# Opening a fused attention and dense kernel with a quarter of q loaded in fp32 by SyncE, k by heads, and both z groups ahead of kv

## The chip, the cores and the metric

The kernel runs on one core of a Trainium2 chip. The metric is the device time of one execution in microseconds (us). Each kernel was executed four or five times, with executions of the kernel before on the same chip in the same rounds. A profile is a trace of one of these executions; its span is about 1.8 us shorter than that execution's time. "Before" and "after" are the two kernels; of the 18 experiments, each has one profile, so a single start or landing time below is that of one execution.

Five engines appear. TensorE multiplies matrices, ScalarE computes exp and tanh, VectorE the other elementwise work; GpSimd and SyncE start loads here. A load is started ("issued") by an engine and carried out by 16 DMA engines; it has "landed" when its data may be used.

## The reference

```python
def phi(x):
    return np.where(x > 0, x, np.exp(x) - 1.0) + 1.0
q_p, k_p = (phi(q), phi(k))                      # q, k, v: (8 batches, 8 heads, 576, 64) fp32
kv = np.einsum('bhsd,bhse->bhde', k_p, v)
z = np.sum(k_p, axis=2)
num = np.einsum('bhsd,bhde->bhse', q_p, kv)
den = np.einsum('bhsd,bhd->bhs', q_p, z)[..., None] + 1e-06
attn = num / den
x = attn.transpose(0, 2, 1, 3).reshape(4608, 512)
h = x @ w_in                                     # 512 x 2048
g = h - np.tanh(h)
out = g @ w_out                                  # 2048 x 512, fp32
```

Linear attention over eight batches gives 4608 tokens; two dense layers follow. phi is computed as min(exp(x), max(x, 0) + 1): an exp on ScalarE, a max and a min on VectorE.

## The kernel before

All inputs are loaded by GpSimd, because they are cast from fp32 to bf16 on the way. They stand in one queue, called the stream here: q, k and v of batch 0 in two halves each, the slices of w_in, then k of batch 1, half of w_out, q of batch 1 (called q(1) here), v of batch 1, the rest of w_out.

```python
def load(b, t, src, halves):
    x = src[b].rearrange("h (p j) d -> (h p) (j d)", j=J)
    if halves:                                   # batch 0: two loads of 256 rows
        for i in range(2):
            nc.gpsimd.dma_start(out=t[:, :, i].rearrange("q h j d -> q h (j d)"),
                                in_=x.rearrange("(h i q) x -> i q h x", h=2, i=2)[i])
    else:
        nc.gpsimd.dma_start(out=t.rearrange("q h i j d -> q (h i) (j d)"), ...)
...
load_q(0)
load_k(0)
make_identity(nc, ident)
load_v(0)
for f0, n in ((0, 256), (256, 256), (512, 512), (1024, 512), (1536, 512)):
    load_wi(f0, n)
load_k(1)
load_wo(0)
load_wo(1)
load_q(1)
...
load_v(1)
load_wo(2)
load_wo(3)
```

The opening computes the attention of batch 0, in this order; `spin` is matmuls on zeros that fill TensorE's waits.

```python
(eq0, rq0, mq0), (eq1, rq1, mq1) = (phi_pieces(0, q_t, qp_t, "qp", i) for i in range(2))
for f in (eq0, rq0, mq0, eq1, rq1, mq1):         # exp, max, min of each half of q
    f()
spin(18)
a_qT_pe(0, 0, side, "AV")                        # transposes of phi(q), first half
...
for f in (ek0, rk0, *ek1, mk0, rk1):
    f()
spin(5)
a_qT_pe(0, 1, side, "AA")
...
b0_z(0)                                          # z of the first half of k
for f in mk1:
    f()
b0_zc(0)                                         # its product with the mask, on VectorE
b0_kv(0)                                         # kv of half the heads; needs v
b0_kz(0)
b0_z(1)                                          # z of the second half of k
b0_zc(1)
a_den(0, Banks([4]))                             # denominators and their reciprocal
...
```

Then come nine chunks of 512 tokens, each with 64 matmuls by w_in and 64 by w_out. In the second layer of the first chunk stand the transposes of phi(q) of batch 1 and, after them, the kv matmuls of batch 1:

```python
s2[3].append(lambda: a_qphi(1, 0))
s2[4].append(lambda: (a_qphi(1, 1), load_q(2), load_k(2), load_v(2)))
...
s2[7].append(lambda: (a_qT_pe(1, 0, side), a_qT_pe(1, 1, side), a_kv(1, side)))
```

## Time and profile before

| what | value |
|---|---|
| time, median of 3 runs | 295.44 us (295.11 to 295.5) |
| span of the profile | 293.2 us |
| TensorE busy | 285.2 us, 97% |
| first dense matmul / start of the long dense run | 16.38 / 17.64 us |
| q(1) landed | 35.92 us |
| kv matmuls of batch 1 start | 39.78 us |

TensorE is the bound, so the opening matters only by how far left it lets TensorE's long run start. The prediction shows the chain of loads, and TensorE at 38 us. The timeline of ScalarE (start, length, engine, line, operation, out<-in, and how many instructions are put together; in brackets the idle time before it and what ended it) tells when the two halves of q land:

```profile
5.55 1.16 ACT L134 ACTIVATE e<-qraw 128x1152 bf16<-128x1152 bf16 x1 [3.32 <-DMA qraw<-in_q_dram]
6.90 1.16 ACT L134 ACTIVATE e<-qraw 128x1152 bf16<-128x1152 bf16 x1 [0.19 <-DMA qraw<-in_q_dram]
```

The timeline of TensorE has the two starts of dense work; between them it makes the last two pairs of batch 0:

```profile
16.38 0.59 PE L366 MATMUL ps_all<-xT,w_in_sb 128*128 128x512 bf16 x2 [0.33 <-DVE xT L244]
16.98 0.73 PE L240 MATMUL ps_all<-rden,sel 32*128 32x128 f32 x16
17.64 13.55 PE L366 MATMUL ps_all<-xT,w_in_sb 128*128 128x512 bf16 x62
```

From 17.64 on TensorE runs without a wait until the transposes at 37.94.

### The profile page before, as it was taken

How to read it: one execution, taken by the hardware profiler on the slowest of the kernel's cores; microseconds unless marked ns; L12 is line 12 of the kernel's file. 1: busy time of each engine (PE TensorE's matmuls, PEld its weight loads, DVE VectorE, ACT ScalarE, POOL GpSimd, SP SyncE). 2: the span in 40 equal slices, each digit the busy share in tenths (PEclk: the TensorE clock that was granted, in tenths of full speed). 3: DMA queues.
4: the chain of work that ended last, by engine and by line, in shares of the span. 5: the costliest groups of instructions: out<-in, count | busy, mean ns of one | idle time of the engine just before them, and what ended most of it. 6: DMA issues, size and time to landing. Idle time of an engine off the chain costs nothing.

```text
span 293.2 us, 4504 instructions
## 1 busy us (share of the span) xinstructions
PE 285.2 (97%) x1801; PEld 134.3 (46%) x1801; DVE 174.6 (60%) x265; ACT 139.6 (48%) x168; POOL 33.3 (11%) x55
## 2 busy tenths in 40 slices
PE   8899999999999999999999999999999999999994
PEld 2544453454444444444444445444444444444443
DVE  4759857887567764786478646865581456106600
ACT  4938536947344643455246524661552155126411
POOL 8673030030030003000300020000000000000000
PEclk9999999999999999999999999999999999999999
DMA  6999999998999758955895669667117310131032
GB/s 101 194 204 212 208 207 216 200 145 153 234 163 185 160 118 139 218 117 129 136 223 127 139 134 183 134 154 143 38 24 178 73 36 0 38 84 24 0 74 72
DMA packets 39077, 38.94 MB, mean 133 GB/s; under 512 B 16336, under 2 KB 33808, under 8 KB 38288
## 3 DMA queue, kind: packets, MB, share of 16 engines
q0 software_dynamic: 17552, 18.35, 38.6%
q1 hardware_dynamic: 21344, 20.17, 30.3%
q8 instruction: 14, 0.23, 0.3%
q10 hardware_dynamic: 160, 0.13, 0.1%
q14 instruction: 7, 0.06, 0.1%
HBM read 43.91 MB, written 9.55 MB: 182 GB/s over the span
## 4 chain that ended last, share of the span: by engine, by line
PE 79%; DMA 11%; issue 7%; POOL 2%; DVE 0%; ACT 0%; POOLq 0%
PE ps_all L387 37%; PE ps_all L366 36%; DMA qraw<-in_q_dram 6%; DMA w_in_sb<-in_moe_w_in_dram 3%; PE ps_all L199 2%; DMA kraw<-in_k_dram 2%; PE ps_all L317 2%; PE ps_all L604 1%; PE ps_all L276 1%; POOL qraw L90 0%; ACT e L134 0%; POOL kraw L93 0%; DVE qp L136 0%; POOL v L93 0%; POOL w_out_sb L115 0%
## 5 line engine op out<-in xcount | busy, mean ns | idle before, releaser
L366 PE MATMUL ps_all<-xT,w_in_sb 128*128 128x512 bf16 x576 | 128.0, 379 | 0.3 <-DVE xT L244 0.3
L387 PE MATMUL ps_all<-w_out_sb,gT 128*128 128x512 bf16 x560 | 127.8, 379 | 0.0
L373 DVE TENSOR_TENSOR gT<-ps_all,th 128x1024 bf16<-128x1024 f32 x64 | 77.9, 1218 | 59.8 <-ACT th L372 59.8
L372 ACT ACTIVATE th<-ps_all 128x1024 f32<-128x1024 f32 x64 | 65.5, 1024 | 57.0 <-PE ps_all L366 47.1
L366 PEld LDWEIGHTS <-w_in_sb 128*128 128x128 bf16 x576 | 55.3, 98 | 66.6 <-issue 0.6
L387 PEld LDWEIGHTS <-gT 128*128 128x128 bf16 x560 | 54.1, 98 | 64.3 <-issue 0.3
L396 ACT COPY osb<-ps_all 128x512 f32<-128x512 f32 (+1 forms) x36 | 20.9, 583 | 73.4 <-PE ps_all L387 54.2
L328 DVE TENSOR_TENSOR xT<-ps_all,rdb 128x512 bf16<-128x512 f32 x24 | 16.3, 689 | 13.4 <-PE ps_all L317 11.2
L134 ACT ACTIVATE e<-qraw 128x1152 bf16<-128x1152 bf16 x16 | 18.5, 1162 | 6.9 <-DMA qraw<-in_q_dram 6.9
L134 ACT ACTIVATE e<-kraw 128x1152 bf16<-128x1152 bf16 x15 | 17.5, 1166 | 0.2 <-DMA kraw<-in_k_dram 0.2
L136 DVE TENSOR_TENSOR qp<-e,r 128x1152 bf16<-128x1152 bf16 x16 | 12.0, 757 | 7.8 <-ACT e L134 7.2
L136 DVE TENSOR_TENSOR kp<-e,r 128x1152 bf16<-128x1152 bf16 x15 | 11.4, 759 | 8.3 <-ACT e L134 7.5
L383 POOL COPY g<-qT 1x1 bf16<-1x1 bf16 x5 | 1.2, 240 | 120.6 <-DMA qT<-qp 120.6
L378 DVE TENSOR_TENSOR gT<-ps_all,th 128x512 bf16<-128x512 f32 x16 | 10.3, 685 | 2.4 <-ACT th L377 1.7
L377 ACT ACTIVATE th<-ps_all 128x512 f32<-128x512 f32 x16 | 9.2, 598 | 4.3 <-PE ps_all L366 3.1
L317 PE MATMUL ps_all<-qT,kz 128*128 128x512 bf16 x28 | 10.1, 379 | 0.0
L444 PE MATMUL ps_all<-zero 128*128 128x512 bf16 x29 | 8.8, 463 | 1.2 <-DVE zero L405 1.2
L135 DVE TENSOR_SCALAR r<-qraw 128x1152 bf16<-128x1152 bf16 x16 | 7.3, 453 | 2.2 <-DMA qraw<-in_q_dram 2.2
L199 PE MATMUL ps_all<-vp,kp 64*128 64x136 bf16 x216 | 7.4, 220 | 0.4 <-POOL g L383 0.4
L199 PEld LDWEIGHTS <-kp 64*128 64x128 bf16 x216 | 6.4, 94 | 3.0 <-issue 2.1
L285 DVE RECIPROCAL rden<-den 128x144 f32<-128x144 f32 x7 | 7.4, 1053 | 0.2
L394 DVE COPY osb<-ps_all 128x128 f32<-128x128 f32 x1 | 0.3, 292 | 11.6 <-PE ps_all L604 11.6
(82 smaller groups left out, 121.7 us busy)
## 6 DMA issues: line engine op xcount, KB each, us to landing
out_dram<-osb SPq DMA_DIRECT2D x70, 128.0 KB
rdb<-ds SPq DMA_DIRECT2D x12, 576.0 KB
kraw<-in_k_dram POOLq DMA_DIRECT2D x7, 576.0 KB, 7.1
qraw<-in_q_dram POOLq DMA_DIRECT2D x7, 576.0 KB, 9.0
v<-in_v_dram POOLq DMA_DIRECT2D x7, 576.0 KB, 12.2
w_out_sb<-in_moe_w_out_dram POOLq DMA_DIRECT2D x4, 512.0 KB, 16.4
w_in_sb<-in_moe_w_in_dram POOLq DMA_DIRECT2D x6, 256.0 KB, 8.6
qraw<-in_q_dram POOLq DMA_DIRECT2D x2, 288.0 KB, 4.6
```

The lines of the kernel that those rows point to most:

```text
L134: return (lambda: nc.scalar.activation(e, x, AF.Exp), lambda: nc.vector.tensor_scalar(r, x, 0.0, 1.0, ALU.max, ALU.add), lambda: nc.vector ...
L136: lambda: nc.vector.tensor_tensor(y, e, r, ALU.min))
L199: nc.tensor.matmul(ps[hg][:, i, :], kp[r, i, j].rearrange("p h d -> p (h d)"), vp[r, i, j, :], start=(j == 0), stop=(j == J - 1))
L317: nc.tensor.matmul(ps, kz[:, p // 2, p % 2, 0:128], qT[:, p % 2, 0:8, p // 2, :], start=True, stop=True)
L328: nc.vector.tensor_mul(xT[:, p, S * b:S * b + 512].rearrange("p (j t c) -> p j t c", j=8, t=4), ps.rearrange("p j (t c) -> p j t c", t=4), ...
L366: nc.tensor.matmul(h, w_in_sb[:, 2 * (p % 2) + p // 2, fi * 128:(fi + 1) * 128], xT[:, p, c * 512:(c + 1) * 512], start=(n == 0), stop=(n ...
L372: nc.scalar.activation(th, h, AF.Tanh)
L373: nc.vector.tensor_sub(gT[:, fi:fi + 2, :], h, th)
L377: nc.scalar.activation(th, h, AF.Tanh)
L378: nc.vector.tensor_sub(gT[:, fi, :], h, th)
L387: nc.tensor.matmul(o, gT[:, fi, i * 128:(i + 1) * 128], w_out_sb[:, fi, :], start=(fi == 0), stop=(fi == NF - 1))
L396: nc.scalar.copy(osb[:, f0:f1], o[:, f0:f1])
```

## The change

The intent is to start phi(q) earlier, with a piece that an idle engine loads while GpSimd has not yet begun, and to take the wait for v out of the way of the denominators. A quarter of q (128 of 512 rows of batch 0) is loaded by SyncE in fp32 into a buffer that is free until the first dense layer. GpSimd's first load is the other quarter of that half. The second half of k becomes two loads, by heads. phi(q)'s first half is done in two pieces. Both z groups and their mask products come before kv.

```diff
@@ load
+                if t is k_t.get(0) and i == 1:
+                    for h in range(2):
+                        nc.gpsimd.dma_start(out=t[:, h, i].rearrange("q j d -> q (j d)"),
+                                            in_=x.rearrange("(h i q) x -> h i q x", h=2, i=2)[h, i])
+                    continue
+                if t is q_t.get(0) and i == 0:
+                    nc.sync.dma_start(out=q_f, in_=x.rearrange("(h i q) x -> h i q x", h=2, i=2)[0, 0])
+                    nc.gpsimd.dma_start(out=t[:, 1, i].rearrange("q j d -> q (j d)"),
+                                        in_=x.rearrange("(h i q) x -> h i q x", h=2, i=2)[1, 0])
+                    continue
... (phi_pieces: exp, max and min by pieces)
@@ opening
+    q_f = gpool.tile([128, NF, 512], BF16, name="gT").rearrange("p a b -> p (a b)").bitcast(F32)[:, 0:J * D]
...
-    for f in (eq0, rq0, mq0, eq1, rq1, mq1):
+    for f in (eq0[0], rq0[0], eq0[1], rq0[1], *mq0, eq1, rq1, mq1):
         f()
-    spin(18)
+    spin(14)
...
-    for f in (ek0, rk0, *ek1, mk0, rk1):
+    for f in (ek0, rk0, *ek1, mk0):
         f()
...
-    spin(6)
+    spin(5)
     b0_z(0)
-    for f in mk1:
-        f()
+    for h in range(2):
+        rk1[h]()
+        mk1[h]()
     b0_zc(0)
+    b0_z(1)
+    b0_zc(1)
     b0_kv(0)
     b0_kz(0)
-    b0_z(1)
-    b0_zc(1)
     a_den(0, Banks([4]))
```

## The prediction

> **What bounds the kernel now.** I began with the page's busy shares: TensorE is at 97% of the span. The timeline of TensorE shows where the other 3% is: after the first dense matmuls it hardly stops until the last outputs, so a change in the opening can only shift that long run to the left. The question is what fixes its place. So I read the chain of work that ended last, in order of time, for the first 60 us:
>
> ```profile
> 1.24 1.33 POOL qraw L90 x2
> ...
> 2.78 6.16 DMA kraw<-in_k_dram
> ...
> 9.22 9.06 DMA w_in_sb<-in_moe_w_in_dram
> ...
> 18.57 0.74 POOL w_out_sb L115
> ...
> 19.39 16.51 DMA qraw<-in_q_dram
> ...
> 35.92 1.17 ACT e L134
> 37.12 0.76 DVE qp L136
> ```
>
> The columns are start, length, what. From 2.78 to 35.92 us it is nearly all loads: the opening, and the first dense stage too, hang on the stream of loads that GpSimd issues, of which the last that matters is q of batch 1, landing at 35.92. I checked this against TensorE's timeline at that place:
>
> ```profile
> 33.83 4.26 PE L387 MATMUL ps_all<-w_out_sb,gT 128*128 128x512 bf16 x19
> 37.94 0.68 PE L164 MATMUL ps_all<-ident,qp 128*128 128x128 bf16 x9
> 39.17 0.68 PE L164 MATMUL ps_all<-ident,qp 128*128 128x128 bf16 x9 [0.56 <-DVE qp L136]
> ```
>
> TensorE arrives at the first transposes of batch 1 at 37.94; their input was ready at 37.88. The second nine wait 0.56 us for the second half of phi(q). So slack here is zero, and the place of everything after 39.17 is the landing of q(1) plus 3.25 us of exp, max, min. The third view is the busy time by windows (the last four columns that matter are the clock, the DMA share and GB/s):
>
> ```profile
> 2.50:2.75 0.25, 0.25 (x2) 0.10 (x1) 0.21 (x7) 0.00 (x0) 0.25 (x1) 1.00 0.00 0
> 2.75:3.00 0.25, 0.25 (x2) 0.12 (x1) 0.25 (x3) 0.00 (x0) 0.25 (x2) 1.00 1.05 60
> 3.00:3.50 0.50, 0.50 (x3) 0.18 (x2) 0.35 (x5) 0.00 (x0) 0.50 (x2) 1.00 0.66 30
> 3.50:4.00 0.50, 0.50 (x3) 0.15 (x1) 0.00 (x0) 0.00 (x0) 0.50 (x2) 1.00 0.89 147
> 4.00:4.50 0.50, 0.50 (x2) 0.15 (x1) 0.00 (x0) 0.00 (x0) 0.45 (x2) 1.00 1.22 210
> ...
> 30.00:34.00 4.00, 4.00 (x20) 1.80 (x19) 3.90 (x8) 2.54 (x5) 0.00 (x0) 1.00 1.22 208
> 34.00:38.00 4.00, 4.00 (x20) 1.72 (x19) 2.94 (x13) 2.08 (x2) 0.00 (x0) 1.00 1.22 206
> ```
>
> Nothing moves before 2.75, little until 3.5, and from 4 us to 38 us the rate is flat at about 205 GB/s. It is a full pipe: q(1) lands when all that was queued ahead of it has passed. The rate counts bf16 written; the loads cast, so about 410 GB/s of fp32 is read.
>
> **What the Trainium skill says.** "DMA: Bandwidth & Descriptors", section "SWDGE vs HWDGE vs iDMA": a DMA that casts must come from GpSimd. This is why the quarter of q that SyncE loads has to stay fp32. The same page, "Specifications": first-byte latency about 1 us from GpSimd, 0.6 us from SyncE or ScalarE, and a fabric ceiling of 435 GB/s. The trace has 1.5 us from GpSimd (issue 1.24, first bytes in the window from 2.75) and 1.1 us for the last output (issued by SyncE at 288.99, bytes in the window from 290.00); the order agrees, the sizes are larger, and I use the trace's. The 410 GB/s read agrees with a pipe near that ceiling. Same page, "Issuing engines are not separate DMA queues": all issuers share the 16 engines and interleave. So SyncE brings no bandwidth here; it can only fill time in which the engines are empty. "VectorE: DVE Perf Modes", "The perf-mode tier table": tensor_scalar on fp32 drops from the 4x to the 2x mode; no instruction of before's profile shows this one.
>
> **The change part by part.**
>
> (1) Quarter of q by SyncE. 128 rows of 2304 bytes, read and written as fp32, in place of 128 rows that GpSimd's stream would have read and cast. In read bytes the pipe carries the same; written bytes go up by 144 KB, which I take as free because the flat rate looks read-bound. One such quarter takes 144 KB / 205 GB/s = 0.72 us of the pipe. The first instructions of the other engines start at 0.73 (ScalarE) to 0.86 (VectorE), GpSimd's DMA at 1.24. If SyncE issues at 0.75 to 0.9, its bytes start at about 1.9 to 2.3, 0.5 to 0.9 us before GpSimd's 2.78, and ramp through the empty stretch up to 3.5. Full hiding is worth 0.72 us, hiding half of it 0.36; with a ramp of its own of some 0.8 us (2.75 to 3.5 for GpSimd's) I take 0.6 us. Every later load, q(1) among them, then lands 0.6 us earlier: q(1) at 35.3.
>
> (2) k of the second half by heads. Two DMAs of 144 KB for one of 288. GpSimd's issue costs 0.74 us for 288 KB and, I estimate, about 0.6 us for a small one, so some 0.5 us more of issue; the issue of v (4.77) is far ahead of its landing (11.89), so it is hidden. The gain is that the first exp of that half may start before all has landed.
>
> (3) phi(q) first half in two pieces: exp 0.67 us each (as the two pieces of k, mean 675 ns) for 1.16, so 0.18 us more on ScalarE; the VectorE max in two pieces, the fp32 one about 0.35 us, min twice 0.42 for 0.76: some 0.2 us more. They start earlier than the 5.55 of now by 0.9 us or more, so this is hidden.
>
> (4) Both z groups ahead of kv. In before kv waits until 11.89 for v, and holds the second z back: z 12.39, its mask product 12.95 to 13.16, reciprocal 13.58. With loads 0.6 us earlier: k first half 8.35; exp to 9.5; min to 10.3; then VectorE runs max 0.25 and min 0.42 twice, to 11.6. Second z 11.6 to 12.0, kv (v landed at 11.3) to 12.45, the 20 denominator matmuls 0.25 + 0.4 to 13.1. Reciprocal 13.1 against 13.58; and 2.80 us from there to the first dense matmul as now: 15.9 against 16.38. The opening itself gains about 0.5 us. The order alone gains nothing unless k is ready before v lands, because the 0.45 us of kv then merely follows.
>
> (5) Five spins fewer (4 + 1): they only fill waits; 0.22 us each when warm, so 14 end near 6.2, where I expect the transposes.
>
> The sum is not (1) + (4): the opening's 0.5 us and the stream's 0.6 us meet at 37.94 to 39.17. TensorE comes there 0.5 us earlier, q(1) 0.6 us earlier; the second transposes still wait for it (gap 0.56 to about 0.46), and the net is the gain of q(1)'s landing, 0.6 us. Beyond 39.17 everything is relative to TensorE. 295.44 - 0.6 = 294.84.
>
> **Rivals.** (a) The opening's whole gain counts, 1 us or more: the removed waits (0.4 for v, 0.4 of the reciprocal for the denominator, the split of k) add up, and the time is 294.2. Against it: zero slack at 37.94; TensorE's gain beyond q(1)'s is returned there as a longer wait. (b) The SyncE load starts late: its first DMA is cold, and the write of the reciprocals issued at 14.66 needed until 20.14 for its readers to go, under load. Then the stream still loses 128 rows but phi(q) waits for SyncE; gain 0 to 0.3, time 295.2 to 295.4. For it: only unloaded cases at the end show 1.1 us. (c) VectorE becomes the opening's bound through eight small pieces in place of five, or the fp32 rows cost the pipe double, 0.7 us: then both are lost and the time is 295.4 to 295.7. Against: both sit in a phase with idle VectorE, and the pipe's rate follows read bytes.
>
> **Range and chances.** The three runs of before spread over 0.4 us, so I can tell 0.6 from 0 only just. (b) and (c) set the high end, 295.4; (a) with a fully hidden quarter the low end, 294.2. Two per cent is 5.9 us, ten times anything in this argument: "within 2%" is nearly certain.
>
> **What would show it.** Right: bytes moving by 2.3 us; the first exp at about 4.3 and not 5.55; the first dense matmul near 15.9; q(1) landed at 35.3; the transposes of batch 1 again waiting for phi(q), and everything after moved by the landing's gain. Wrong: q(1) landing at 35.9 in spite of an early SyncE load (the pipe is not read-bound), or the transposes of batch 1 without a wait (then the opening sets the end), or new gaps of TensorE between 16 and 38 us, at a dense matmul whose weights came late.

## The result, and the profile after

The changed kernel took 295.69 us (median of 4 runs, 295.27 to 296.19); the kernel before 295.27 in the same rounds (4 runs). The ratio is 1.0017, with a 95% interval of 0.9996 to 1.0039. A ratio is always the mean time of one kernel's runs over that of the other's runs of the same rounds, so it isn't quite the ratio of the medians. "Within 2%" held. The predicted gain of 0.6 us did not come, and 295.69 lies above the predicted range.

The chain of work that ended last, after, for the first 60 us (start, length, what):

```profile
1.91 6.18 DMA qraw<-in_q_dram
8.11 1.17 ACT e L147
9.31 0.76 DVE qp L149
...
13.40 0.39 PE ps_all L223 x18
13.79 0.53 PE ps_all L234 x18
...
18.91 2.49 PE ps_all L379 x11
```

Before, this chain ran through loads up to q(1) at 35.92. Now it leaves the loads at 8.11, with the second half of q, and goes through the opening's compute into the dense run. In the page's shares of the chain by engine the loads fall from 11% of the span to 4% (first before, then after):

```profile
PE 79%; DMA 11%; issue 7%; POOL 2%; DVE 0%; ACT 0%; POOLq 0%
PE 77%; issue 7%; DVE 6%; DMA 4%; ACT 3%; POOL 1%; SPq 0%; DVEq 0%; ACTq 0%; POOLq 0%
```

So something else bounds the start than the prediction had. ScalarE's timeline says where it begins:

```profile
3.77 0.68 ACT L143 ACTIVATE e<-gT 128x576 bf16<-128x576 f32 x1 [1.54 <-DMA gT<-in_q_dram]
5.45 0.68 ACT L143 ACTIVATE e<-qraw 128x576 bf16<-128x576 bf16 x1 [1.00 <-DMA qraw<-in_q_dram]
8.11 1.16 ACT L147 ACTIVATE e<-qraw 128x1152 bf16<-128x1152 bf16 x1 [1.98 <-DMA qraw<-in_q_dram]
...
35.47 2.22 ACT L147 ACTIVATE e<-qraw 128x1152 bf16<-128x1152 bf16 x2 [1.73 <-DMA qraw<-in_q_dram]
```

The SyncE quarter is there at 3.77, earlier than predicted. But the second half of q, which GpSimd loads, comes at 8.11 and not at 6.90: 1.21 us later, although a quarter of q has been taken out of the stream in front of it. Much further down the same stream, q(1) lands at 35.47, 0.45 us earlier than before. TensorE's timeline answers both:

```profile
17.58 0.38 PE L379 MATMUL ps_all<-xT,w_in_sb 128*128 128x512 bf16 x1 [0.33 <-DVE xT L257]
18.18 0.73 PE L253 MATMUL ps_all<-rden,sel 32*128 32x128 f32 x16 [0.23 <-DVE xT L257]
18.84 13.55 PE L379 MATMUL ps_all<-xT,w_in_sb 128*128 128x512 bf16 x61
32.23 7.07 PE L400 MATMUL ps_all<-w_out_sb,gT 128*128 128x512 bf16 x31
39.14 1.17 PE L177 MATMUL ps_all<-ident,qp 128*128 128x128 bf16 x18
40.37 1.66 PE L190 MATMUL ps_all<-v,kp 64*128 64x192 bf16 x36
```

The start of the dense work is 1.20 us later (17.58 for 16.38, 18.84 for 17.64). The eighteen transposes of batch 1 now run in one piece, with no wait for phi(q): the gap of 0.56 us is gone, because q(1) came early and TensorE late. So 1.20 of delay less about 0.6 of gap leave the kv matmuls of batch 1 at 40.37 instead of 39.78, 0.59 us later, and the span is 0.6 us longer.

The two profiles suggest a rule for the start of these kv matmuls: the later of *long dense run + 21.52* (after: 18.84 + 21.52 = 40.36) and *q(1) landing + 3.86* (before: 35.92 + 3.86 = 39.78). The constants were read from these two profiles. In both, the span is that start plus 253.4. The experiments will test it.

The windows of the two kernels (window, its length, busy time of PE, PEld, DVE, ACT and POOL with their counts, clock, DMA share, GB/s written) show what the stream did. Before:

```profile
2.50:3.50 1.00, 1.00 (x4) 0.40 (x3) 0.82 (x12) 0.00 (x0) 1.00 (x3) 1.00 0.59 30
3.50:4.50 1.00, 1.00 (x4) 0.30 (x2) 0.00 (x0) 0.00 (x0) 0.95 (x3) 1.00 1.05 179
4.50:8.00 3.50, 3.21 (x19) 1.43 (x18) 1.59 (x3) 2.26 (x2) 3.47 (x6) 1.00 1.17 190
8.00:12.00 4.00, 3.55 (x47) 1.98 (x46) 3.20 (x7) 3.45 (x6) 2.07 (x4) 1.00 1.19 198
```

After:

```profile
2.50:3.50 1.00, 1.00 (x4) 0.40 (x3) 0.82 (x12) 0.00 (x0) 1.00 (x3) 1.00 0.95 242
3.50:4.50 1.00, 1.00 (x4) 0.30 (x2) 0.46 (x1) 0.68 (x1) 1.00 (x3) 1.00 1.06 146
4.50:8.00 3.50, 2.77 (x20) 1.40 (x19) 1.15 (x3) 0.68 (x1) 3.06 (x6) 1.00 1.09 147
8.00:12.00 4.00, 2.32 (x31) 1.10 (x30) 2.96 (x6) 3.89 (x6) 2.44 (x4) 1.00 1.18 195
```

The empty time before 3.5 us is filled, as intended. But from 4.5 to 8 us the rate is 147 GB/s and not 190. That is 43 GB/s x 3.5 us = 150 KB not moved, about what the quarter of q (144 KB in bf16) had saved the stream; that the two are so near is chance, as the second profile of the same kernel shows (159 GB/s, so 109 KB). The column before the rate is the time that the DMA engines' packets took, as a share of the window. It falls only from 1.17 to 1.09 while the rate falls from 190 to 147, so in after the same bytes took about a fifth more packet time. That speaks against engines that merely had nothing to move.

The trace's packet records show one thing more. A load ends with sixteen 4-byte packets, and the Trainium skill ("DMA: Bandwidth & Descriptors", section "Why a DMA increments its semaphore by 16 and not by 1") says that for a load from GpSimd each of the 16 DMA engines posts a completion, and that the load has landed only when all have. In before the sixteen completions of GpSimd's first load lie within 0.35 us. In after fourteen lie within 0.46 us, and the next two come 1.31 and 1.46 us after the first. So the consumers seem to wait for one or two engines that lag by about a microsecond. The records don't name the engine, so which completion belongs to which load is read from their order. Where an engine lags by more than a whole load this order fails: in after the 32nd completion, which would be the last of GpSimd's second load, comes at 7.17, but the exp that needs that load starts only at 8.11, where in before it starts 0.3 to 0.4 us after its load's last completion.

### The profile page after: what moved, and what is told of

It is laid out like the page before. It is cut to its first block, busy times and chain, and to the rows that moved or that the text cites. A ratio compares the mean times of both kernels' runs of the same rounds, so it can differ in the third digit from the quotient of the medians.

```text
span 293.8 us, 4473 instructions
## 1 busy us (share of the span) xinstructions
PE 281.9 (96%) x1767; PEld 133.5 (45%) x1796; DVE 175.5 (60%) x268; ACT 139.5 (47%) x169; POOL 33.5 (11%) x56
## 4 chain that ended last, share of the span: by engine, by line
PE 77%; issue 7%; DVE 6%; DMA 4%; ACT 3%; POOL 1%; SPq 0%; DVEq 0%; ACTq 0%; POOLq 0%
PE ps_all L379 36%; PE ps_all L400 34%; DVE gT L391 2%; PE ps_all L212 2%; DMA out_dram<-osb 2%; DMA qraw<-in_q_dram 2%; PE ps_all L330 2%; ACT th L390 1%; PE ps_all L289 1%; DVE r L148 1%; ACT osb L409 1%; DVE kp L149 1%; DVE qp L149 1%; PE ps_all L253 0%; SPq L414 0%
## 5 line engine op out<-in xcount | busy, mean ns | idle before, releaser
L400 PE MATMUL ps_all<-w_out_sb,gT 128*128 128x512 bf16 x547 | 126.3, 379 | 0.7
L147 ACT ACTIVATE e<-qraw 128x1152 bf16<-128x1152 bf16 x15 | 17.3, 1162 | 3.7 <-DMA qraw<-in_q_dram 3.7
L149 DVE TENSOR_TENSOR qp<-e,r 128x1152 bf16<-128x1152 bf16 x15 | 11.3, 757 | 6.9 <-ACT e L147 6.2
L459 PE MATMUL ps_all<-zero 128*128 128x512 bf16 x24 | 7.3, 458 | 1.2 <-DVE zero L418 1.2
```

The costliest lines, as they stand in the source:

```text
L147: return (lambda: nc.scalar.activation(e, x, AF.Exp), lambda: nc.vector.tensor_scalar(r, x, 0.0, 1.0, ALU.max, ALU.add), lambda: nc.vector ...
L149: lambda: nc.vector.tensor_tensor(y, e, r, ALU.min))
L400: nc.tensor.matmul(o, gT[:, fi, i * 128:(i + 1) * 128], w_out_sb[:, fi, :], start=(fi == 0), stop=(fi == NF - 1))
```

## The experiments

All 18 runs gave correct results.

### e1: the change again

The unchanged file of after, to see how far one profile stands for the kernel.

> The changed kernel again, unedited, for a second profile. Theory S (the SyncE load disturbs GpSimd's stream) and theory H (loads of 128 rows instead of 256 are slow): the pattern repeats: second half of q lands after 7.7 us (before: 6.9), the first dense matmul starts near 17.6 (before: 16.4), q of batch 1 lands at 35.3 to 35.6, time 0.2 to 0.6 us over before. Theory A (an accident of the one profiled execution): second half of q by 6.9, first dense matmul near 16.

Measured: 295.48 us against 294.96; ratio 1.0016 (1.0000 to 1.0031). Of what was expected for a repeated pattern only the time held (0.2 to 0.6 us over). This execution's second half of q was there at 7.10, not 8.11, short of the expected 7.7 but still 0.2 us later than before, and the rate from 4.5 to 8 us was 159 GB/s. The long dense run began at 17.91, q(1) landed at 35.72, and kv began at 39.57: by the rule max(39.43, 39.58). So the delay of the opening differs between executions (the profiled one, 294.74, was the fastest of its four), the slower time of the rounds hardly does: two sets put the kernel 0.16% and 0.17% above before. Their intervals begin at 1.0000 and 0.9996, so neither excludes a tie by itself. That the predicted gain of 0.2% is absent is shown; that there is a loss is likely; its size is not shown.

### e2: the order of z and kv alone

```diff
# against the kernel before
     b0_zc(0)
-    b0_kv(0)
-    b0_kz(0)
     b0_z(1)
     b0_zc(1)
+    b0_kv(0)
+    b0_kz(0)
     a_den(0, Banks([4]))
```

> The kernel before with the order of the z and kv groups alone changed. All theories of the loads: q and k land as in before (6.9, 8.9, 10.5); kv now follows the second z, so the reciprocal starts 0 to 0.2 us later than 13.58 and the first dense matmul at 16.4 to 16.6. Because the transposes of batch 1 wait for q of batch 1 (gap 0.56 in before), the time is that of before within 0.15 us. If the order itself were the loss (rival O), the first dense matmul would be near 17.6.

Measured: 294.95 us against 294.96; 1.0001 (0.9986 to 1.0016). The reciprocal starts at 13.71 instead of 13.58, the first dense matmul at 16.51 instead of 16.38. The order alone costs the opening 0.13 us, which is not seen in the time.

### e3: k by heads alone

```diff
# against the kernel before
+                if t is k_t.get(0) and i == 1:
+                    for h in range(2):
+                        nc.gpsimd.dma_start(out=t[:, h, i]..., in_=...[h, i])      # as in the change
+                    continue
...
-    for f in (ek0, rk0, *ek1, mk0, rk1):
+    for f in (ek0, rk0, *ek1, mk0):
...
-    for f in mk1:
-        f()
+    for h in range(2):
+        rk1[h]()
+        mk1[h]()
```

> The kernel before with the second half of k in two loads of 128 rows (and max and min in two pieces), alone. Theory S: loads as in before, second half of q at 6.9, first dense matmul at 16.0 to 16.5, time as before within 0.2 us. Theory H: the small loads pull slowly: k later than 10.5 by 0.5 us or more and the first dense matmul at 16.9 or later.

Measured: 294.73 us against 294.96; 0.9995 (0.9979 to 1.0012). Second half of q at 6.87 as before; reciprocal 13.21, first dense matmul 16.01, so 0.37 us earlier in the opening. The stream is not disturbed (198 GB/s from 4.5 to 8 us). But TensorE waits for q(1) as before:

```profile
37.62 0.68 PE L169 MATMUL ps_all<-ident,qp 128*128 128x128 bf16 x9
38.85 0.68 PE L169 MATMUL ps_all<-ident,qp 128*128 128x128 bf16 x9 [0.56 <-DVE qp L141]
39.46 1.66 PE L182 MATMUL ps_all<-v,kp 64*128 64x192 bf16 x36
```

kv begins at q(1)'s 35.60 + 3.86 = 39.46, to the hundredth. This part is harmless, and what it gains in the opening is held back by q(1), as the prediction had it. Note that q(1) itself came 0.32 us earlier than before, without any SyncE load.

### e4: the quarter by GpSimd instead of SyncE

```diff
# against the kernel after
-                    nc.sync.dma_start(out=q_f, in_=x.rearrange("(h i q) x -> h i q x", h=2, i=2)[0, 0])
-                    nc.gpsimd.dma_start(out=t[:, 1, i].rearrange("q j d -> q (j d)"),
-                                        in_=x.rearrange("(h i q) x -> h i q x", h=2, i=2)[1, 0])
+                    for h in range(2):
+                        nc.gpsimd.dma_start(out=t[:, h, i].rearrange("q j d -> q (j d)"),
+                                            in_=x.rearrange("(h i q) x -> h i q x", h=2, i=2)[h, 0])
```

> The changed kernel with the quarter of q taken back from SyncE: GpSimd loads it with the cast, as one load of 128 rows ahead of the other. Theory S: second half of q back at 6.9 to 7.1, first dense matmul at 16.0 to 16.5, q of batch 1 at 35.9 as in before, time as before within 0.2 us. Theory H: second half of q still after 7.7 us, first dense matmul 17.2 or later, time 0.3 us or more over before.

Measured: 296.19 us against 294.96; 1.0048 (1.0027 to 1.0070). Slower than both. The second half of q came at 7.49, the first dense matmul at 17.58 as in after, and q(1) only at 37.85. So without SyncE the opening is as late as with it, and the saving further down the stream is gone too. The SyncE load cannot be the only cause of the delay.

### e5: the SyncE quarter of q alone

```diff
# against the kernel before: the q part of the change's load, q_f, and
-    for f in (eq0, rq0, mq0, eq1, rq1, mq1):
+    for f in (eq0[0], rq0[0], eq0[1], rq0[1], *mq0, eq1, rq1, mq1):
```

> The kernel before with the q part of the change alone (a quarter in fp32 by SyncE, the other quarter of that half as a GpSimd load of 128 rows). Theory Q (breaking q's first load in two slows the stream behind it until about 8.5, whoever loads the pieces): second half of q lands at 7.1 to 8.1 as in the changed kernel, k later than before, first dense matmul 16.7 to 17.6, time 0.2 to 0.7 us over before. Rival K (it takes the split of k behind it as well): second half of q by 6.3, time as before or 0.4 us under.

Measured: 295.17 us against 294.95; 1.0008 (0.9993 to 1.0023). Second half of q at 7.45, first dense matmul 16.94, rate from 4.5 to 8 us 154 GB/s, q(1) at 36.40. The delay belongs to the q part of the change; k by heads and the order of z are not needed for it. And q(1), which this part was to bring forward by 0.6 us, landed 0.48 us later than before (35.92):

```profile
36.40 2.22 ACT L144 ACTIVATE e<-qraw 128x1152 bf16<-128x1152 bf16 x2 [3.09 <-DMA qraw<-in_q_dram]
```

### e8: a SyncE quarter that nobody uses

The kernel before, with the same SyncE load added; q is still loaded whole by GpSimd. This isolates what the transfer does to its neighbours.

```diff
# against the kernel before
+    q_f = gpool.tile([128, NF, 512], BF16, name="gT").rearrange("p a b -> p (a b)").bitcast(F32)[:, 0:J * D]
+    nc.sync.dma_start(out=q_f, in_=q[0].rearrange("h (p j) d -> (h p) (j d)", j=J)[0:128])
     load_q(0)
```

> The kernel before, all of its loads as they were, with the same fp32 quarter loaded by SyncE in addition and never used. Theory Q: GpSimd's stream runs as in before; SyncE's bytes move from 1.8 to 3.3 us in the empty stretch; q at 5.5 and 6.9, k at 8.9, give or take 0.3; the time within 0.2 us of before. Theory S (an early SyncE load disturbs the stream): rate below 170 GB/s between 4 and 8.5 us, second half of q after 7.3, time 0.3 us or more over before.

Measured: 295.32 us against 294.95; 1.0014 (0.9997 to 1.0030). The start of the stream is late by 1.2 us:

```profile
6.74 1.16 ACT L134 ACTIVATE e<-qraw 128x1152 bf16<-128x1152 bf16 x1 [4.51 <-DMA qraw<-in_q_dram]
8.15 1.16 ACT L134 ACTIVATE e<-qraw 128x1152 bf16<-128x1152 bf16 x1 [0.25 <-DMA qraw<-in_q_dram]
```

Yet the rate from 4.5 to 8 us is 192 GB/s, as before. The packet records have the rest: fifteen of the first load's sixteen completions lie within 0.33 us, the sixteenth comes 1.43 us after the first. By that order the load is nearly all there, and one engine holds up phi(q). The stream as a whole hardly suffers: q(1) lands at 36.02. Each theory got half: the landing is late, as theory S had it, at theory Q's rate.

### e9: GpSimd's three quarters in one load

```diff
# against the kernel after
-                    nc.gpsimd.dma_start(out=t[:, 1, i].rearrange("q j d -> q (j d)"),
-                                        in_=x.rearrange("(h i q) x -> h i q x", h=2, i=2)[1, 0])
-                    continue
+                    nc.gpsimd.dma_start(out=t.rearrange("q h i j d -> q (h i) (j d)")[:, 1:4],
+                                        in_=x.rearrange("(n q) x -> q n x", n=4)[:, 1:4])
+                    return
```

> The changed kernel with the three quarters of q that GpSimd loads put in one load of 384 rows instead of one of 128 and one of 256. Theory Q: no small load at the head of the stream, so the rate stays near 200 GB/s from 3.5 us; all of q landed at 5.7 to 6.2; k at 8.2 to 8.5; first dense matmul at 15.6 to 16.1; q of batch 1 at 35.2 to 35.5; time 0.4 to 0.7 us under before. Theory S: still slow, second half of q after 7.0, time at or over before.

Measured: 295.73 us against 294.95; 1.0027 (1.0003 to 1.0051). The dip of the rate is gone (193 GB/s from 4.5 to 8 us), so the small load has to do with it; that much of theory Q held. The opening is not better, though: all three quarters have to land before phi(q) goes on, at 8.04, and the first dense matmul comes at 18.55. q(1) lands at 35.69, and the rule's first term decides: 19.81 + 21.52 = 41.33, measured 41.33.

### e10: the SyncE quarter on k instead of q

```diff
# against the kernel before: a quarter of k's first half by SyncE into k_f, GpSimd loads
# the other quarter as one load of 128 rows behind q; k's phi in pieces
+                if t is k_t.get(0) and i == 0:
+                    nc.gpsimd.dma_start(out=t[:, 1, i]..., in_=...[1, 0])
+                    continue
...
+    nc.sync.dma_start(out=k_f, in_=k[0].rearrange("h (p j) d -> (h p) (j d)", j=J)[0:128])
     load_q(0)
```

> The kernel before with SyncE loading a quarter of k (not of q) in fp32 ahead of everything, so that GpSimd's first two loads, of q, stay whole. Theory Q: q lands as in before (5.5, 6.9), k's first half at 8.2 to 8.4 instead of 8.9, the rest 0.6 us earlier, q of batch 1 at 35.2 to 35.4, and the time 0.4 to 0.7 us under before: the gain that the prediction promised, by the same pipe argument. Theory S: stream slow between 4 and 8.5, time at or over before.

Measured: 294.58 us against 294.95; 0.9990 (0.9975 to 1.0005). q was late again, at 6.58 and 7.99, with three of sixteen completions 1.22 to 1.45 us behind the first; the half of the idea that meant to spare q failed. q(1) landed at 35.38, the earliest of the kernels that load it whole, and kv began at 39.57 (18.04 + 21.52 = 39.56). The two effects of a SyncE quarter are seen side by side: the opening later, the stream earlier.

### e11: the unused quarter, and early work on it

An exp and a max on the unused quarter as soon as it has landed, to see whether the early work on ScalarE and VectorE disturbs GpSimd's loads.

```diff
# against e8's kernel (the unused SyncE quarter)
+    nc.scalar.activation(g_f[:, 2048:2048 + J * D], q_f, AF.Exp)
+    nc.vector.tensor_scalar(g_f[:, 4096:4096 + J * D], q_f, 0.0, 1.0, ALU.max, ALU.add)
```

> The run with the extra, unused SyncE quarter, plus exp on ScalarE and max on VectorE over that quarter as soon as it has landed (results unused): the early work of the changed kernel without any change of GpSimd's loads. Theory L (an early SyncE load makes some of the 16 DMA engines start GpSimd's stream late, and nothing more): rates from 4 to 8.5 us as in the extra run, 180 to 210 GB/s, first q at 6.3 to 6.8, time within 0.2 us of the extra run (1.0014). Theory C (work of ScalarE or VectorE at 3.7 us, while GpSimd writes descriptors, slows the stream): a dip below 130 GB/s between 3.5 and 5 us and the first q 0.4 us or more later than in the extra run, as in the changed kernel.

Measured: 295.78 us against 294.96; 1.0028 (1.0013 to 1.0043). The halves of q at 6.00 and 7.79, q(1) at 36.73. So the same unused quarter delays the first half by 0.45 us here and by 1.19 in the run above. The ratio is higher than with the unused quarter alone (the intervals overlap), but the stream's dip in this execution (76 GB/s from 3.0 to 3.5 us) came before the early work began, so it isn't shown to come from that work. A cleaner test follows below.

### e12: half of the unused quarter

```diff
# against e8's kernel
-    nc.sync.dma_start(out=q_f, in_=q[0].rearrange("h (p j) d -> (h p) (j d)", j=J)[0:128])
+    nc.sync.dma_start(out=q_f[:, 0:288], in_=q[0].rearrange("h (p j) d -> (h p) (j d)", j=J)[0:128, 0:288])
```

> The extra SyncE load cut to half its columns (rows of 1152 bytes), so that it is over by about 2.7 us, before GpSimd's stream starts at 2.8 to 3. Theory L with overlap as the cause: no engine late, first q at 5.5 and second at 6.9 as in before, time within 0.2 us of before. If an early load alone does it, whether or not it overlaps: first q still at 6.2 or later, time 0.3 us over.

Measured: 294.85 us against 294.96; 0.9997 (0.9981 to 1.0014). With half the columns the transfer is over before GpSimd's begins, and it costs the opening nothing:

```profile
5.54 1.16 ACT L134 ACTIVATE e<-qraw 128x1152 bf16<-128x1152 bf16 x1 [3.31 <-DMA qraw<-in_q_dram]
6.96 1.16 ACT L134 ACTIVATE e<-qraw 128x1152 bf16<-128x1152 bf16 x1 [0.26 <-DMA qraw<-in_q_dram]
```

All sixteen completions of the first load are within 0.33 us again. (Its own completions end at 2.63 us; the stream's first packet starts at 2.79. The full quarter's end at 3.33.) So a second issuer as such does no harm. That the overlap with the start of GpSimd's stream does it fits both runs, but size and row length were halved together with it, and no run separates them.

### e16: half of the unused quarter, with early work

```diff
# against e12's kernel
+    for n in (0, 1):
+        nc.scalar.activation(g_f[:, 2048:2048 + 288], q_f[:, 0:288], AF.Exp)
+        nc.vector.tensor_scalar(g_f[:, 4096:4096 + 288], q_f[:, 0:288], 0.0, 1.0, ALU.max, ALU.add)
```

> The run with the extra half quarter (which was as fast as before), plus two exp on ScalarE and two max on VectorE over it from about 3 us on, results unused. Theory C: the stream dips, first q at 5.9 or later, second at 7.4 or later, time 0.3 us or more over. Otherwise q at 5.5 and 6.9 to 7.0 and the time as before within 0.2 us: early work is harmless.

Measured: 295.07 us against 295.10; 1.0001 (0.9988 to 1.0015). The halves of q at 5.37 and 6.83, as early as in any kernel that loads them whole, with the exp running from 2.98. Early compute on half a piece does not make the loads late.

### e15: the first half of q as two GpSimd loads

No SyncE, no work in pieces: only the load is cut.

```diff
# against the kernel before
+                if t is q_t.get(0) and i == 0:
+                    for h in range(2):
+                        nc.gpsimd.dma_start(out=t[:, h, i].rearrange("q j d -> q (j d)"),
+                                            in_=x.rearrange("(h i q) x -> h i q x", h=2, i=2)[h, i])
+                    continue
```

> The kernel before, with the first half of q loaded by GpSimd as two loads of 128 rows and nothing else changed (phi of that half still waits for both). Theory P (two small loads at the head of the stream slow what is behind them): second half of q at 7.3 or later against 6.9, k after 9.4, first dense matmul 16.8 or later, time 0.3 us or more over. Theory C (it was the early exp and max): q at 5.3 and 6.9, first dense matmul at 16.3 to 16.5, time as before within 0.2 us.

Measured: 296.25 us against 295.10; 1.0038 (1.0021 to 1.0055). This single cut makes the kernel slower than before:

```profile
5.67 1.16 ACT L139 ACTIVATE e<-qraw 128x1152 bf16<-128x1152 bf16 x1 [3.43 <-DMA qraw<-in_q_dram]
8.36 1.16 ACT L139 ACTIVATE e<-qraw 128x1152 bf16<-128x1152 bf16 x1 [1.53 <-DMA qraw<-in_q_dram]
```

The first half is hardly later, the second 1.46 us. The window from 4.5 to 8 us:

```profile
4.50:8.00 3.50, 2.77 (x17) 1.25 (x16) 1.22 (x2) 1.16 (x1) 3.42 (x8) 1.00 1.03 137
```

137 GB/s against 190: the dip of after, without SyncE. Here it is not made up: q(1) lands at 37.41, 1.49 us late. GpSimd had issued the second half of q at 2.42, over five us before it landed, so its issue was not late. The completions, by their order, are spread here too: those of the second half of q over 1.86 us (6.12 to 7.98), where before's lie within 0.30. So engines that finish unevenly are not a mark of the SyncE load alone, and the two causes may have one mechanism.

### e19: the second half of q as two GpSimd loads

```diff
# against e15's kernel
-                if t is q_t.get(0) and i == 0:
+                if t is q_t.get(0) and i == 1:
```

> Kernel before with the second half of q, not the first, as two GpSimd loads by heads. Theory (small loads hurt only at the head of the stream, where the next load has little lead): first q as before (5.4 to 5.6), second q at 6.9 to 7.2, k at 8.9 to 9.3, first dense matmul 16.3 to 16.6, time within 0.2 us of before. Rival (any split of a q load costs over 1 us, wherever it stands): k at 10 or later, first dense matmul at 17.4 or later, time 0.7 to 1.2 us above before.

Measured: 295.53 us against 294.85; 1.0017 (1.0002 to 1.0032). The opening is not disturbed: q at 5.52 and 7.00, first dense matmul 16.28.

```profile
4.50:8.00 3.50, 3.50 (x20) 1.56 (x19) 1.73 (x3) 2.16 (x2) 3.42 (x8) 1.00 1.20 199
```

So the same cut one place further down the stream leaves the rate at 199 GB/s. What the theory expected of the opening held, the time did not: it is 0.7 us above before by the medians. q(1) at 36.05 instead of 35.92 explains 0.13 us of the profiled execution (39.91 = 36.05 + 3.86); the rest is not explained.

### e20: the second half of q first, then the small load

```diff
# against the kernel after
+                    nc.gpsimd.dma_start(out=t[:, :, 1].rearrange("q h j d -> q h (j d)"),
+                                        in_=x.rearrange("(h i q) x -> i q h x", h=2, i=2)[1])
                     nc.gpsimd.dma_start(out=t[:, 1, i].rearrange("q j d -> q (j d)"),
                                         in_=x.rearrange("(h i q) x -> h i q x", h=2, i=2)[1, 0])
-                    continue
+                    break
...
-    for f in (eq0[0], rq0[0], eq0[1], rq0[1], *mq0, eq1, rq1, mq1):
+    for f in (eq0[0], rq0[0], eq1, rq1, mq1, eq0[1], rq0[1], *mq0):
```

> Kernel after with GpSimd's first two q loads exchanged: the second half of q (256 rows) goes first, the small quarter second, and the pieces of phi(q) in the same order. If the small load at the head is the larger of the two costs in after: k lands by 9.3 (after 9.76), first dense matmul 16.6 to 17.1 (after 17.58), span 293.0 to 293.3, time 0.2 to 0.6 us below after. If the SyncE load beside GpSimd's first load is the larger cost whatever stands first: the second half lands at 6.5 or later, k at 9.7 or later, first dense matmul 17.3 to 17.8, time as after.

Measured: 296.47 us against 294.85; 1.0070 (1.0039 to 1.0101). (One of its four executions, with the lowest clock, 0.986, took 298.09; the others 296.24 to 296.64.) Neither expectation held. The whole half at the head landed at 5.83, only 0.3 us late beside the SyncE quarter. But the rate dipped all the same, to 156 GB/s from 4.5 to 8 us, with the low stretch from 5.5 on; the small load landed at 7.35, and the first dense matmul came at 18.14. So "a small load hurts only at the head" is too simple: it hurt here in second place, beside a SyncE load, and did not hurt in second place in the run above, without one.

### e13: q(1) in two halves

The rule says that TensorE waits for all of q(1) + 3.86. Two halves let phi(q(1)) begin earlier.

```diff
# against the kernel before
-        load(b, q_t[b], q, b == 0)
+        load(b, q_t[b], q, b <= 1)
```

> A version meant to beat both: the kernel before with q of batch 1 loaded in two halves, so that its first phi does not wait for all of it. By the rule that all runs so far obey (the kv matmuls of batch 1 start at the later of long dense run + 21.52 us and landing of q of batch 1 + 3.86 us), the second term falls by about 1.2 us and the first, 17.64 + 21.52 = 39.16, takes over from 39.78: time 0.6 us under before (294.3 to 294.5). If the rule is wrong, or the extra load costs as much as it saves: no change.

Measured: 294.91 us against 294.96; 0.9999 (0.9984 to 1.0014). The first half of q(1) was there at 35.16, and the transposes ran without a wait. The dense run started at 17.98 in this execution, so kv began at 39.50 = 17.98 + 21.52, and the 0.6 us that were expected did not come. A new wait stands behind it:

```profile
39.50 1.66 PE L177 MATMUL ps_all<-v,kp 64*128 64x192 bf16 x36
41.45 1.02 PE L387 MATMUL ps_all<-w_out_sb,gT 128*128 128x512 bf16 x3 [0.28 <-DMA w_out_sb<-in_moe_w_out_dram]
```

The same stream brings the third quarter of w_out, and TensorE has caught up with it. The stream is a third bound, 0.3 us behind the other two.

### e14: k by heads and q(1) in two halves

```diff
# e3's diff and e13's together, against the kernel before
```

> The same with k of batch 0 split by heads as well, which alone brought the long dense run to 17.26 without any gain in time beyond 0.3 us: now 17.26 + 21.52 = 38.78 against 39.78 in before, so 1.0 us under before (293.9 to 294.1), unless v or w_out of the same stream becomes the wait.

Measured: 294.79 us against 294.96; 0.9997 (0.9982 to 1.0012). kv at 39.22, 0.56 us earlier than before; of that, 0.26 us are given back at once to the wait for w_out, and the span is 292.9, 0.3 us less. The expected 1.0 us was missed by far.

### e17: k by heads, and 256 columns of a k quarter by SyncE

A version built from what did no harm: a small SyncE load that is over early, and cuts only behind q.

```diff
# against the kernel before, with e3's diff
+                if t is k_t.get(0) and i == 0:
+                    nc.sync.dma_start(out=k_f, in_=x[0:128, 0:256])
+                    nc.gpsimd.dma_start(out=t[:, 0, 0, 4:J].rearrange("q j d -> q (j d)"), in_=x[0:128, 256:J * D])
+                    nc.gpsimd.dma_start(out=t[:, 1, 0].rearrange("q j d -> q (j d)"), in_=x[256:384])
+                    continue
...
+    nc.scalar.copy(k_t[0][:, 0, 0, 0:4].rearrange("q j d -> q (j d)"), k_f)
```

> The kernel with k split by heads, in which SyncE also loads 256 columns of a quarter of k in fp32 at the very start (over by about 2.6 us, before GpSimd's stream starts), ScalarE copies them to bf16 and GpSimd loads the rest. If what the prediction got wrong is only the overlap: q as in before (5.5, 6.9), all behind it 0.32 us earlier (128 KB of fp32 read, 64 KB of bf16, at 205 GB/s), q of batch 1 near 35.3 to 35.6, and the time 0.4 to 0.6 us under before, of which the split of k alone gave 0.15 to 0.23. If small loads or early work matter here too: no better than the split of k alone.

Measured (5 rounds): 294.70 us against 295.10; 0.9986 (0.9972 to 1.0000). q at 5.45 and 6.88, rate 203 GB/s from 4.5 to 8 us, first dense matmul 16.05, q(1) 35.58, kv 39.43. Here GpSimd's third and fourth loads are small, and nothing dips.

### e18: the same with q(1) in two halves

```diff
# e17's diff and e13's together, against the kernel before
```

> The same with q of batch 1 in two halves. The wait for the third quarter of w_out (0.26 us in the runs with the two halves) moves 0.3 us earlier with the stream, so the long dense run alone sets the place: kv matmuls of batch 1 at 38.8 to 39.1 and the time 0.6 to 0.9 us under before.

Measured (5 rounds): 294.68 us against 295.10; 0.9987 (0.9975 to 1.0000). kv at 39.40, where 38.8 to 39.1 was expected, then a wait of 0.59 us for w_out, which was to be out of the way. These two are the best versions found, 0.13% to 0.14% faster than before with intervals that end at 1.0000. That is at the edge of what such rounds can tell, the more so for the best two picked out of many, and no version here is shown to be an improvement.

### All runs side by side

Times of the profiled executions in us; "q" is the start of the exp on the first and on the last piece of q that GpSimd loads; GB/s from 4.5 to 8 us; the last three columns are the start of the long dense run, q(1)'s landing (its first half, where it is loaded in halves), and the start of kv of batch 1.

| kernel | ratio | q, first / last | GB/s | long dense run | q(1) | kv |
|---|---|---|---|---|---|---|
| before | 1 | 5.55 / 6.90 | 190 | 17.64 | 35.92 | 39.78 |
| e2, z order alone | 1.0001 | 5.49 / 6.96 | 184 | 17.77 | 35.90 | 39.75 |
| e3, k by heads alone | 0.9995 | 5.46 / 6.87 | 198 | 17.26 | 35.60 | 39.46 |
| e12, unused half quarter | 0.9997 | 5.54 / 6.96 | 189 | 17.74 | 36.24 | 40.09 |
| e16, with early work | 1.0001 | 5.37 / 6.83 | 180 | 17.73 | 36.00 | 39.85 |
| e13, q(1) halves | 0.9999 | 5.54 / 6.95 | 183 | 17.98 | 35.16 | 39.50 |
| e14, k by heads, q(1) halves | 0.9997 | 5.45 / 6.89 | 194 | 17.70 | 34.36 | 39.22 |
| e17, k part by SyncE | 0.9986 | 5.45 / 6.88 | 203 | 17.30 | 35.58 | 39.43 |
| e18, the same, q(1) halves | 0.9987 | 5.59 / 7.02 | 201 | 17.88 | 34.79 | 39.40 |
| e19, second half of q cut | 1.0017 | 5.52 / 7.00 | 199 | 17.54 | 36.05 | 39.91 |
| **after** | 1.0017 | 5.45 / 8.11 | 147 | 18.84 | 35.47 | 40.37 |
| e1, after again | 1.0016 | 4.39 / 7.10 | 159 | 17.91 | 35.72 | 39.57 |
| e4, quarter by GpSimd | 1.0048 | 4.46 / 7.49 | 160 | 18.84 | 37.85 | 41.71 |
| e5, q part alone | 1.0008 | 5.47 / 7.45 | 154 | 18.20 | 36.40 | 40.25 |
| e8, unused quarter | 1.0014 | 6.74 / 8.15 | 192 | 18.28 | 36.02 | 39.88 |
| e11, unused quarter, early work | 1.0028 | 6.00 / 7.79 | 195 | 18.30 | 36.73 | 40.58 |
| e9, three quarters in one | 1.0027 | 8.04 / 8.62 | 193 | 19.81 | 35.69 | 41.33 |
| e10, SyncE quarter of k | 0.9990 | 6.58 / 7.99 | 167 | 18.04 | 35.38 | 39.57 |
| e15, first half of q cut | 1.0038 | 5.67 / 8.36 | 137 | 19.02 | 37.41 | 41.26 |
| e20, half first, then small | 1.0070 | 5.83 / 7.35 | 156 | 19.40 | 35.63 | 40.92 |

Two things are seen here. The rule for kv holds in all twenty profiles within 0.02 us (with q(1) in halves its first term alone decides), and the span is that start plus 253.3 to 254.0. And the kernels can be put in two groups by the last piece of q: ten profiles have it by 6.83 to 7.02, ten at 7.10 to 8.62. The border is narrow (7.10 is the second profile of after, which has a quarter of q less in front of it). The late ones are exactly those with a full SyncE quarter at the start, or with q's first half cut into small GpSimd loads at the head, or both.

## Why the prediction was wrong, point by point

**What bounds the kernel.** Right in kind: the place of TensorE's long run is set where the opening meets q(1), at the transposes and kv of batch 1, and the gain of one side is returned as a wait for the other. All twenty profiles agree with this. The prediction's "slack here is zero" also told that the other side would take over at once; it looked only at the case that the stream stays last.

**Step (1), the quarter of q by SyncE.** This is the step that failed. It held that SyncE "can only fill time in which the engines are empty" and that "every later load, q(1) among them, then lands 0.6 us earlier". SyncE was in fact earlier than assumed (exp at 3.77, estimated 4.3). But the second half of q landed 1.21 us later (8.11 against 6.90, predicted about 6.3) in one profile of after and 0.20 in the other. At the end of the stream q(1) landed 0.45 and 0.20 us earlier in the two, not 0.6. Even this gain is not shown to be SyncE's: with the q part alone (e5) q(1) came 0.48 us later, with k by heads alone (e3) 0.32 earlier; only the SyncE quarter of k (e10) had it 0.54 earlier by itself. Four kernels whose GpSimd loads are the same (before, e2, e12, e16) have it at 35.90 to 36.24, which is the spread to reckon with. So neither "only fill" nor "every later load" held. Two terms were missing from the sum:

- A SyncE quarter that still moves when GpSimd's stream begins: shown by the unused quarter, which makes the first q late by 1.19 us (6.74 against 5.55) in one run and 0.45 in the other, and by half of it, which costs nothing. The rate from 4.5 to 8 us does not fall (192 and 195 GB/s). In after and in four of the runs with a full SyncE quarter (e5, e8, e9, e10) one to three of the sixteen completions of the first load lag; in e1, e11 and e20 they don't.
- A small GpSimd load at the head: shown by cutting q's first half and nothing else, which makes the second half 1.46 us late, at 137 instead of 190 GB/s.

The changed kernel does both. The two effects don't add up (1.21 in all), and the runs don't tell what share each has in it, or whether they are one effect.

Under this step lay the picture of a pipe that is flat at about 205 GB/s from 4 us on. Its table shows 4.0 to 4.5 us and 30 us on; in between, before has 190 GB/s from 4.5 to 8 and 198 from 8 to 12, so the early stream was not the steady one that the sum of 0.72 us took it for. And the 435 GB/s that it sets beside the reads stands on that page for the SBUF side, where these loads write 205 GB/s; so that the reads set the rate was not shown by it, and no run here tests it.

**Step (2), k by heads.** Right that its issue is hidden, and better than said: alone it brought the first dense matmul 0.37 us forward (16.01 against 16.38).

**Step (3), phi(q) in pieces.** Right that it is hidden. The fp32 max was estimated at 0.35 us and took 0.46, where the same size in bf16 takes 0.33 (VectorE's timeline); it ran in an idle stretch.

```profile
3.77 0.46 DVE L144 TENSOR_SCALAR r<-gT 128x576 bf16<-128x576 f32 x1 [0.28 <-DMA gT<-in_q_dram]
5.45 0.33 DVE L144 TENSOR_SCALAR r<-qraw 128x576 bf16<-128x576 bf16 x1 [1.22 <-DMA qraw<-in_q_dram]
```

**Step (4), both z groups ahead of kv.** It rested on step (1)'s earlier loads for most of its 0.48 us, so it fell with it: the reciprocal came at 14.78, not 13.1. Its own part was mis-sized too. From the exp on the second half of q to the reciprocal, before needs 13.58 - 6.90 = 6.68 us and after 14.78 - 8.11 = 6.67. k by heads alone needs 13.21 - 6.87 = 6.34, so the order of z took back the 0.34 us that k by heads gained. The lines show how (kv is `v,kp`, z is `one,kp`; before, then after): in before kv runs while VectorE still makes the second phi(k), at no cost; in after TensorE waits 1.20 us for that phi(k), runs z at 13.40, then kv from 13.64, and only then the denominators.

```profile
11.89 0.68 PE L221 MATMUL ps_all<-v,kp 64*128 64x128 bf16 x18 [0.45 <-DMA v<-in_v_dram]
12.39 0.40 PE L210 MATMUL ps_all<-one,kp 64*128 64x32 bf16 x18
```

```profile
13.40 0.39 PE L223 MATMUL ps_all<-one,kp 64*128 64x32 bf16 x18 [1.20 <-DVE kp L146]
13.64 0.66 PE L234 MATMUL ps_all<-v,kp 64*128 64x128 bf16 x18
```

The prediction's "kv merely follows" is this, but it counted it as neutral. That the order alone costs 0.13 us in the opening is measured.

**Step (5), the spins.** Harmless in both versions; nothing hung on them.

**The sum.** "The second transposes still wait for it ... and the net is the gain of q(1)'s landing" is where the wrong step came out. The wait of 0.56 us disappeared because TensorE was 1.20 us late. With the measured terms the same sum gives max(18.84 + 21.52, 35.47 + 3.86) = 40.36, which is 0.58 us after before's 39.78; the spans differ by 0.6. In the second profiled execution of after the sum gives 39.58 and the span is 293.0, 0.2 us less than before's. The medians of the two sets of rounds are 0.4 and 0.5 us above before.

**The rivals.** (a) was ruled out rightly for its reason: TensorE's gain beyond q(1)'s would have been returned. (b) was wrong, SyncE was early. (c) has the measured 295.69 in its range (295.4 to 295.7), by luck more than by its mechanism: the fp32 rows did not cost the pipe double in after (q(1) was early there). VectorE's pieces do stand in the chain behind the second half of q, up to the 1.20 us wait above, but that stretch took no longer than in before (6.67 us against 6.68). The prediction's own test named the outcome, "the transposes of batch 1 without a wait (then the opening sets the end)", without giving it a chance in the range.

**What stays open.** Why some engines lag by about 1.1 to 1.4 us, and why small loads near the head lower the rate for several us in six kernels (137 to 167 GB/s) but not in five others that cut loads in second to sixth place (194 to 203 GB/s). Early compute is not needed for it (e15 has none) and did no harm on half a piece (1.0001). That the next load is prepared too late after a small one would be a guess: the traces show the issues in time (in e15 over five us ahead) and the packets longer rather than missing (share 1.03 at 137 GB/s, against 1.17 at 190). That the time is up 0.6 to 0.7 us with the second half of q cut, where the opening is undisturbed, is unexplained too.

## What to carry to other kernels

When the start of a long run is the later of two chains, write the prediction as a maximum of both with each of the change's terms in each, and ask for every transfer what it does to its nearest neighbours, not only to the end of the queue: here, in one profile, the end of the stream gained 0.45 us while its head lost 1.21. A load is as late as its last engine, so mean bandwidth does not tell when it lands (in e8 the rate was 192 GB/s and the first load 1.19 us late). One profile is one execution: the same kernel's next one had 0.20 us for the 1.21. Before building on a helper load, add it unused to the old kernel, then at half the size: two runs of a few lines separated its cost from all else.

## What the Trainium skill lacked or had wrong

- "DMA: Bandwidth & Descriptors", section "Issuing engines are not separate DMA queues", says that loads of several issuers interleave and that issuing from several engines only saves issue time. It gives no size for how far the interleaving can hold up the other stream's first load: an unused 288 KB SyncE load moved it from 5.55 to 6.74 us (to 6.00 in another run), and half of that load did not (5.54).
- The same page says that two of the 16 engines are usually slower than the others, but has no time for how far apart the 16 finish one load: in ten undisturbed profiles within 0.26 to 0.42 us, but up to 1.46 us apart when a full SyncE quarter overlapped the first load.
- No page found has, beyond general advice to make transfers large, the cost of cutting a load at the head of a stream: two loads of 128 rows for one of 256 lowered the rate from 190 to 137 GB/s for 3.5 us and cost 1.0038 (1.0021 to 1.0055) in time, while cuts into such loads further down left the rate at 194 to 203 GB/s in five kernels without a full SyncE quarter.
- "DMA: Bandwidth & Descriptors", section "Specifications": the first-byte latencies (about 1 us from GpSimd, 0.6 us from SyncE) don't say from where they count. From the start of the issuing instruction the traces show more. In slices of 0.225 us SyncE's first bytes fall between 1.58 and 1.80 us with the issue at 0.74, so 0.8 to 1.1 us later; GpSimd's, in before, between 2.70 and 2.93 with the issue at 1.24, so 1.5 to 1.7 us. From the end of that instruction (by the trace 0.43 us long on SyncE, 0.84 on GpSimd) it is 0.4 to 0.6 and 0.6 to 0.9 us, so near the page, which is not shown to be wrong.
- "VectorE: DVE Perf Modes", "The perf-mode tier table": fp32 in a lower mode than bf16 agrees in direction. The page's own times for 2048 elements (1227 and 693 ns) are in a ratio of 1.8; at 128x576 here they are 0.46 and 0.33 us, a ratio of 1.4. So the table's modes are not ratios of times for short instructions; nothing is shown to be wrong.
